# Transposing the packed queries of six batches with one crossbar transfer in place of twelve PE transposes

## The chip, the cores and the metric

One core of a Trainium2 chip. The metric is device time of one execution in microseconds (us), less is better; medians are over single executions, and each execution also reports the mean clock that was granted to TensorE (1.00 is full speed). "PE" is TensorE's matmul side, DVE VectorE, ACT ScalarE, POOL GpSimd, SP the engine whose queue issues the output writes and the crossbar transposes here. A "crossbar transfer" is here a DMA that transposes bf16 data on its way from SBUF to SBUF. A transfer has landed with the last of its sixteen semaphore updates in the trace (counted here as one for each DMA engine).

## The reference, cut to what matters

```python
# q, k, v: (8, 8, 576, 64); p: (8, 8, 32, 64)  (batch, heads, sequence, head size)
p_packed = sm_attn(p, k, v)            # 32 packed queries attend to 576 keys
out      = sm_attn(q, p_packed, p_packed)   # 576 queries attend to 32 packed rows
x = out.transpose(0, 2, 1, 3).reshape(4608, 512)
h = x @ w_in; g = h * np.cos(h); result = g @ w_out      # 512 -> 2048 -> 512
```

For the first product the kernel needs p transposed, head size on the partitions: this is the tile `P2`, for all eight batches. It is a small tensor (8 x 8 x 32 x 64).

## The kernel before

The kernel is a software pipeline over batches. Slot `s` does the feed-forward part of batch `s` (16 steps `fc` of `h_mm`), fills PE with output matmuls of batch `s-1` ("fillers"), and runs pieces of the attention of the next batches as hooks at given steps. All this is one stream of PE instructions.

```python
    def xbar(n, b):                                   # q or k of batch b, by the crossbar
        t = xT[n, b] = att_pool.tile([128, H * 3, TP], BF16, ..., bufs=2 if n == "k" else 1)
        nc.sync.dma_start_transpose(out=t, in_=bf[n, b].rearrange("p h x -> p (h x)"))

    def pack_p(b0, b1, flat=None):                    # p of batches b0..b1-1, by PE
        ng = 2 * (b1 - b0)
        if flat is None:
            flat = psa(BF16).rearrange("p a x -> p (a x)")
        for g in range(ng):
            nc.tensor.transpose(flat[:, g * 128:(g + 1) * 128],
                                p_bf[:, 2 * b0 + g].rearrange("p t d -> p (t d)"), ident)
        V.tensor_copy(out=P2[:, b0:b1].rearrange("p b h n -> p (b h n)"), in_=flat[:, 0:ng * 128])

    # a1_xbar(b): crossbar transfer of the softmax weights a1 of batch b -> a1T[b]
    # pp(b):      PE product of a1T[b] with v of batch b; ppw(b, n): its product with w_in
    # [cut]
    def next_loads():
        G.tensor_copy(out=gate, in_=xT["k", 3][0:1, 0, 0:1])     # POOL waits until kT of batch 3 is there
        for n, b in (("q", 3), ("k", 4), ("v", 3)):
            load(n, b)

    # [cut]
    load("q", 2)
    load("k", 3)
    dup_p(4, 2 * B, G)                                # POOL casts p to p_bf
    # [cut]
    slot(1, [(3, lambda: pw2(1, 2, (ACT, V))), (4, lambda: (xbar("q", 2), xbar("k", 3))), (5, tk("k", 2, 0)), (6, tk("k", 2, 1)),
             (7, tk("k", 2, 2)), (9, lambda: pack_p(2, 5)),
             (11, lambda: pack_p(5, B)), (12, next_loads)], 4, {3: 3})
    # [cut]  s1(2), pp(2), s2(2), s1(3), then:
    xbar("q", 3)
    a1_xbar(3)
    recips(3)
    xbar("k", 4)
    # [cut]
    slot(2, [(7, lambda: pp(3, engs=(ACT, ACT))), (11, lambda: pw2(3))], 5, {11: 3})

    for s in range(3, B):                             # [cut] the same chain, once per slot
        ...
        slot(s, [(5, lambda: pp(s + 1, engs=(ACT, ACT))), (10, lambda: pw2(s + 1))] if nxt else [], 5, {10: 3})
```

The softmax here doesn't subtract the row's maximum and nothing guards it: scores larger than these inputs give would overflow.

## Time and profile before

| | before |
|---|---|
| time, median of 6 runs | 248.92 us (248.79 to 249.83) |
| span of the profiled run, granted clock | 247.7 us, 1.00 |
| PE busy | 236.7 us, 96% of the span |
| chain of waits that ended last | 74% PE, 15% DMA (first weights) |

From the profile's page: the busy row of all engines, then two of the rows that cut the span into 40 slices (a digit is tenths of busy time; PEclk is the granted clock), then the chain of waits by engine.

```profile
PE 236.7 (96%) x2037; PEld 131.4 (53%) x2037; DVE 167.3 (68%) x253; ACT 166.8 (67%) x278; POOL 57.8 (23%) x70
...
PEclk9999999999999999999999999999999999999999
DMA  5999999999899989999998985999481113101133
...
PE 74%; DMA 15%; DVE 4%; ACT 2%; POOL 2%; issue 1%; DVEq 0%; POOLq 0%
```

PE is the bound. The DMA engines show work in flight nearly all the time up to 150 us, though they are hardly on the chain after 44 us. The two PE places that matter are in PE's timeline (columns: start in us, time in us, engine, line, operation, count; a bracket at the end of a line would be idle time ahead of it):

```profile
56.06 0.65 PE L256 MATMUL psA<-a2n,PPW 128*128 128x288 bf16 x4
56.55 0.50 PE L117 MATMUL psA<-ident,p_bf 128*128 128x128 bf16 x6
56.88 0.59 PE L309 MATMUL ot<-w_out_bf,gT 128*128 128x512 bf16 x2
57.53 0.65 PE L256 MATMUL psA<-a2n,PPW 128*128 128x288 bf16 x4
...
84.42 0.38 PE L309 MATMUL ot<-w_out_bf,gT 128*128 128x512 bf16 x1
84.63 0.65 PE L256 MATMUL psA<-a2n,PPW 128*128 128x288 bf16 x4
85.19 0.86 PE L183 MATMUL psA<-a1T,vp 96*128 96x64 bf16 x24
85.89 0.60 PE L309 MATMUL ot<-w_out_bf,gT 128*128 128x512 bf16 x2
```

The first four lines are step 9 of slot 1: with six transposes (L117) the step takes 57.53 - 56.06 = 1.47 us, where a plain step with two fillers takes 0.92. The last four are pp(3) (L183) in slot 2: no idle time ahead of it. Its first weight load, which overlaps the matmuls before it, starts at 85.00:

```profile
85.00 0.92 PEld L183 LDWEIGHTS <-vp 96*128 96x128 bf16 x24
```

The data for pp(3) comes down the SP queue; its timeline:

```profile
47.64 2.05 SPq L316 DMA_DIRECT2D out_dram<-osb  x4
56.42 3.92 SPq L93 DMA_TRANSPOSE qT<-qbf  x1
60.39 2.94 SPq L93 DMA_TRANSPOSE kT<-kbf  x1
63.43 8.02 SPq L316 DMA_DIRECT2D out_dram<-osb  x6
72.82 6.16 SPq L93 DMA_TRANSPOSE qT<-qbf  x1
79.08 3.56 SPq L156 DMA_TRANSPOSE a1T<-a  x1
82.72 3.10 SPq L93 DMA_TRANSPOSE kT<-kbf  x1
```

The queue sits idle from 49.69 to 56.42, until the load of q2 lands. And POOL's timeline, for the two events that frame this stretch: the cast of p, and the gate that holds back the next loads until kT of batch 3 has landed.

```profile
46.82 1.60 POOL L342 CAST p_bf<-p_raw 128x768 bf16<-128x768 f32 x2 [5.67 <-DMA p_raw<-in_p_dram]
...
65.36 0.18 POOL L443 COPY gate<-kT 1x1 bf16<-1x1 bf16 x1 [8.68 <-DMA kT<-kbf]
```

So there is a second chain beside PE: crossbar of k3 -> gate -> load of q3 -> crossbar of q3 (72.82) -> crossbar of a1 of batch 3 (79.08, its last semaphore update at 84.66) -> pp(3) on PE. It arrives only 0.3 us before PE wants it (84.66 against 85.00).

### The profile page before, as it was taken

The page shows a single profiled execution, that of the slowest core. Times are in us where ns is not written, and L with a number is a line of the kernel's source. Part 1 is how long each engine was busy: PE and PEld are TensorE (multiplying, and loading weights), DVE is VectorE, ACT ScalarE, POOL GpSimd, SP SyncE. Part 2 cuts the span into 40 slices and gives each one's busy share as a digit, 9 for nine tenths or more (in the row PEclk, how much of TensorE's full clock was granted, in tenths as well). Part 3 has the DMA queues.
Part 4 walks back from the last instruction along what each step waited for, and adds up shares of the span by engine and source line. Part 5 has one row for each costly group of instructions (what it writes and reads, how often), then busy time and mean ns, then how long its engine had stood idle before and what let it go on. Part 6 is the DMA issues. An engine that isn't in the chain of part 4 may idle for free.

```text
span 247.7 us, 5071 instructions
## 1 busy us (share of the span) xinstructions
PE 236.7 (96%) x2037; PEld 131.4 (53%) x2037; DVE 167.3 (68%) x253; ACT 166.8 (67%) x278; POOL 57.8 (23%) x70
## 2 busy tenths in 40 slices
PE   8888799999999999999999999999999999999993
PEld 3454374566554654565446554565456554665452
DVE  2449987789667977678767766678766684886110
ACT  2359789756656887888776777888777684873000
POOL 8252543240310455013404005030500000000000
PEclk9999999999999999999999999999999999999999
DMA  5999999999899989999998985999481113101133
GB/s 79 203 202 205 205 206 229 197 241 147 176 186 207 181 146 219 216 204 160 233 185 171 188 178 71 200 165 187 105 154 30 45 42 83 46 27 58 47 83 85
DMA packets 63175, 37.09 MB, mean 150 GB/s; under 512 B 35792, under 2 KB 58576, under 8 KB 63152
## 3 DMA queue, kind: packets, MB, share of 16 engines
q0 software_dynamic: 23152, 18.75, 49.8%
q1 hardware_dynamic: 39568, 17.83, 34.6%
q8 instruction: 16, 0.26, 0.4%
q10 hardware_dynamic: 432, 0.20, 0.4%
q14 instruction: 7, 0.06, 0.1%
HBM read 37.22 MB, written 9.44 MB: 188 GB/s over the span
## 4 chain that ended last, share of the span: by engine, by line
PE 74%; DMA 15%; DVE 4%; ACT 2%; POOL 2%; issue 1%; DVEq 0%; POOLq 0%
PE ot L309 44%; PE psA L256 20%; DMA w_out_bf<-in_moe_w_out_dram 9%; DMA w_in_bf<-in_moe_w_in_dram 7%; PE psA L207 3%; DVE gT L263 2%; PE psA L129 2%; PE psA L183 2%; PE ot L295 1%; ACT cosT L260 1%; PE psA L233 1%; DVE PPW L77 1%; ACT ppT L75 1%; DVE a2n L243 1%; POOL kbf L84 1%
## 5 line engine op out<-in xcount | busy, mean ns | idle before, releaser
L309 PE MATMUL ot<-w_out_bf,gT 128*128 128x512 bf16 x512 | 133.3, 379 | 0.1
L263 DVE TENSOR_TENSOR gT<-psA,cosT 128x576 bf16<-128x576 f32 x128 | 93.7, 756 | 26.6 <-ACT cosT L260 25.9
L260 ACT ACTIVATE cosT<-psA 128x576 bf16<-128x576 f32 x128 | 82.5, 652 | 27.7 <-PE psA L256 24.5
L256 PE MATMUL psA<-a2n,PPW 128*128 128x288 bf16 x512 | 83.9, 286 | 1.4 <-DVE PPW L77 0.4
L309 PEld LDWEIGHTS <-gT 128*128 128x128 bf16 x512 | 47.7, 98 | 43.3 <-issue 6.8
L256 PEld LDWEIGHTS <-PPW 128*128 128x128 bf16 x512 | 49.3, 98 | 34.7 <-issue 3.9
L77 DVE CAST PPW<-psA 128x1024 bf16<-128x1024 f32 (+1 forms) x23 | 26.9, 1176 | 11.6 <-PE psA L207 11.5
L267 POOL COPY joint<-gT 128x512 bf16<-128x512 bf16 x16 | 9.9, 616 | 85.5 <-DVE gT L263 85.5
L77 DVE COPY osb<-ot 128x512 f32<-128x512 f32 (+1 forms) x24 | 16.3, 679 | 17.5 <-PE ot L309 13.9
L77 POOL COPY vp<-vbf 96x3072 bf16<-96x3072 bf16 x7 | 19.3, 2751 | 5.1 <-DMA vbf<-in_v_dram 5.1
L75 ACT COPY osb<-ot 128x512 f32<-128x512 f32 (+1 forms) x13 | 7.3, 565 | 15.3 <-PE ot L309 10.6
L243 DVE SCALAR_TENSOR_TENSOR a2n<-a2u,r,lns 128x576 bf16<-128x576 bf16 x16 | 12.4, 813 | 7.3 <-ACT lns L241 7.3
L235 ACT ACTIVATE lns<-psA 128x576 f32<-128x576 f32 x16 | 10.1, 650 | 7.1 <-PE psA L233 6.5
L140 ACT ACTIVATE a<-psA 128x576 bf16<-128x576 f32 x16 | 10.3, 647 | 6.7 <-PE psA L129 6.7
L309 PE MATMUL ot<-w_out_bf,joint 128*128 128x512 bf16 x48 | 13.0, 379 | 0.0
L225 ACT ACTIVATE a2u<-psA,rs 128x576 bf16<-128x576 f32 x16 | 11.0, 737 | 1.4 <-PE psA L129 1.2
L75 ACT CAST ppT<-psA 64x128 bf16<-64x128 f32 x24 | 6.2, 260 | 6.5 <-DVE ppT L77 5.9
L207 PE MATMUL psA<-w_in_bf,ppT 64*32 64x512 bf16 x224 | 10.2, 381 | 0.0
L241 ACT ACTIVATE lns<-lns 128x576 f32<-128x576 f32 x16 | 10.0, 676 | 0.0
L347 PE MATMUL ot<-wz 128*128 128x512 bf16 x25 | 8.7, 486 | 1.2 <-DVE wz L358 1.2
L84 POOL DMA_DIRECT2D vbf<-in_v_dram x8 | 6.2, 777 | 6.8 <-DVE vp L77 4.8
L77 DVE COPY kT<-psA 128x768 bf16<-128x768 bf16 x8 | 4.2, 552 | 5.1 <-PE psA L104 5.0
(73 smaller groups left out, 150.4 us busy)
## 6 DMA issues: line engine op xcount, KB each, us to landing
kbf<-in_k_dram POOLq DMA_DIRECT2D x8, 576.0 KB, 12.7
vbf<-in_v_dram POOLq DMA_DIRECT2D x8, 576.0 KB, 7.8
qbf<-in_q_dram POOLq DMA_DIRECT2D x8, 576.0 KB, 10.0
out_dram<-osb SPq DMA_DIRECT2D x24, 192.0 KB, 2.5
out_dram<-osb SPq DMA_DIRECT2D x22, 128.0 KB, 2.4
w_in_bf<-in_moe_w_in_dram POOLq DMA_DIRECT2D x4, 512.0 KB, 17.5
w_out_bf<-in_moe_w_out_dram POOLq DMA_DIRECT2D x4, 512.0 KB, 21.2
out_dram<-osb SPq DMA_DIRECT2D x26, 64.0 KB, 2.1
```

The source lines that it names most:

```text
L75: ACT.copy(out=out, in_=in_)
L77: eng.tensor_copy(out=out, in_=in_)
L140: ACT.activation(out=a1[b % 2][:, y, :, 0:TP].rearrange("p (e m) x -> p e m x", e=2), in_=ps[y][:, :, 0:HS].rearrange("p e (m x) -> p e m ...
L207: nc.tensor.matmul(ps[y][32 * x:32 * x + 32, :], ppT[b % 2][r, 2 * x + y, :], w_in_bf[r, x, n * 512:(n + 1) * 512], start=True, stop=True)
L225: ACT.activation(out=a2u[b][:, y].rearrange("p (e x) -> p e x", e=2), in_=ps[y][:, :, 0:HS], func=AF.Exp, scale=rs1[b][:, y:y + 1])
L235: ACT.activation(out=lns[b][:, y].rearrange("p (e x) -> p e x", e=2), in_=ps[:, :, 0:HS], func=AF.Ln)
L241: ACT.activation(out=lns[b][:, y], in_=lns[b][:, y], func=AF.Exp, scale=-1.0)
L243: V.scalar_tensor_tensor(out=a2n[b][:, y], in0=a2u[b][:, y], scalar=r1[b][:, y:y + 1], in1=lns[b][:, y], op0=ALU.mult, op1=ALU.mult)
L256: nc.tensor.matmul(ps[:, e, 0:HS], PPW[b][:, y, fc * 128:(fc + 1) * 128], a2n[b][:, y, e * HS:(e + 1) * HS], start=(y == 0), stop=(y == 1))
L260: ACT.activation(out=csv, in_=ps[:, :, 0:HS], func=AF.Sin, bias=PI_HALF)
L263: V.tensor_tensor(out=gT[b][:, fc, :].rearrange("p (e x) -> p e x", e=2), in0=ps[:, :, 0:HS], in1=csv, op=ALU.mult)
L309: nc.tensor.matmul(pss[c], w, w_out_bf[:, fc, :], start=(fc == 0), stop=(fc == NFC - 1))
```

## The change

p is to be transposed by one crossbar transfer (128 x 1536 elements) in the idle stretch of the SP queue, so that PE is rid of twelve transposes and DVE of two copies from PSUM.

```diff
+    def xbars():
+        nc.sync.dma_start_transpose(
+            out=P2[:, 2:B].rearrange("p b (g h) n -> p (b g) (h n)", g=2),
+            in_=p_bf[:, 4:2 * B].rearrange("p g t d -> p (g t d)"))
+        xbar("q", 2)
+        xbar("k", 3)
+
@@
-    slot(1, [..., (4, lambda: (xbar("q", 2), xbar("k", 3))), (5, tk("k", 2, 0)), (6, tk("k", 2, 1)),
-             (7, tk("k", 2, 2)), (9, lambda: pack_p(2, 5)),
-             (11, lambda: pack_p(5, B)), (12, next_loads)], 4, {3: 3})
+    slot(1, [..., (4, xbars), (5, tk("k", 2, 0)), (6, tk("k", 2, 1)),
+             (7, tk("k", 2, 2)), (12, next_loads)], 4, {3: 3})
```

More of the change, by code (lines that the diff above doesn't have):

```diff
@@ L461 @@
     fill(14)
-    slot(1, [(3, lambda: pw2(1, 2, (ACT, V))), (4, lambda: (xbar("q", 2), xbar("k", 3))), (5, tk("k", 2, 0)), (6, tk("k", 2, 1)),
-             (7, tk("k", 2, 2)), (9, lambda: pack_p(2, 5)),
-             (11, lambda: pack_p(5, B)), (12, next_loads)], 4, {3: 3})
+    slot(1, [(3, lambda: pw2(1, 2, (ACT, V))), (4, xbars), (5, tk("k", 2, 0)), (6, tk("k", 2, 1)),
+             (7, tk("k", 2, 2)), (12, next_loads)], 4, {3: 3})
     ACT.preload_act_table_set(EXP_SET)
```

## The prediction

> **What bounds the kernel now.** The page's busy table has PE at 236.7 us of 247.7 (96%), clock 1.00; the chain of waits is 74% PE, 15% DMA (weight loads before 44 us), 4% DVE. After 44 us PE work counts one to one, unless PE then meets a wait. The DMA row reads 9 in nearly every slice up to 150 us. Beside PE runs a DMA chain with little slack: k's crossbar, the next three loads (gated by kT), q's crossbar, a1's crossbar, pp.
>
> **What goes.** Twelve PE transposes in two hooks of slot 1 (fc 9 and 11). The timeline shows 0.50 us for six of them, and two 0.55 us evictions of P on DVE. Steps with such a hook take 1.47 and 1.52 us, the same without 0.92 us. So PE saves about 1.1 us near 58 to 60 us, on the chain.
>
> **What comes.** One crossbar transfer, 128 x 1536 bf16, an a1 crossbar's size, which the SP timeline shows 1.43 us issuing when quiet, 3.56 us under load; 4.0 us to land. Its source is ready: POOL's cast of p ends at 48.4. The SP queue is idle from 49.7 to 56.42, where q2's crossbar waits for q2's load (waits of the SP queue). So no issue is delayed. s1(2) needs P2 at 64.4; it should land by 60.
>
> The cost is bandwidth. From 44 to 57 us the loads run at a steady 265 packets of 768 B per us: saturated. The new transfer is 1536 packets of 256 B; the trace's crossbars move 800 to 1130 such packets per us alone: I estimate 1.4 to 1.9 us more of all 16 engines ahead of q2's and k3's crossbars. [...] at 77 to 78.5 us, beside crossbar packets, loads fall from 133 to about 90 per half microsecond. Some hides in gaps near 58.5 and 61 us. I take kT3 to land 0.7 to 2 us late (now 65.1), centre 1.3.
>
> **On the critical path.** kT3 itself has 7 us of slack before s1(3) at 72.0. But the next loads are gated by it (POOL waits until 65.36); q3's crossbar issues when q3 lands (72.8), a1's follows at 79.08 and lands near 84.7; pp(3) starts at 85.0. Slack: 0.3 us. With PE 1.1 us earlier and a1T 1.3 us later, PE should stall there about 2 us. Net: -1.1 + (1.1 + 1.3 - 0.3) = +1.0 us. At pp(4) slack exceeds 1 us: nothing more is lost.
>
> **Predicted time: 249.8 us, 248.0 to 251.3** (8 in 10). Faster by over 2%: 0.01; within 2%: 0.96; slower by over 2%: 0.03.
>
> **What would show each step.** Transposes of p on PE down from 16 to 4, steps fc 9 and 11 at 0.92 us; s1(2) near 63.3 instead of 64.39. The new transpose issued near 49.7, issuing for 2 to 4 us; q2's crossbar about 1 us after 56.42. POOL's gate 0.7 to 2 us after 65.36. An idle gap on PE of 1 to 3 us before pp(3), released by the a1T DMA; pp(3) near 86. From there both traces run parallel.
>
> **What would make it wrong.** If the new transfer fits into DMA gaps, the delay is near zero and the kernel gains up to 1 us (248). If it stalls q2's crossbar longer, the loss is 2 to 3 us.

One clause of the recorded text is cut (marked), as no trace of this case shows it. What the trace of the kernel before has: "saturated" is a DMA share of 1.27 (packet times, as a share of 16 engines' time) at 213 GB/s from 44 to 57 us; 768 B packets started at 244 to 270 per us from 45 to 51 us and from 54 to 56, but at 104 to 174 per us between, beside output writes, so they were not steady throughout. "Quiet" is a share of 0.59 during the issue of 1.43 us (at 155.84), "under load" 1.30 during that of 3.56 us (at 79.08). The slack at pp(4) is 1.5 us (a1T of batch 4 lands at 107.46, pp(4) starts at 108.98).

## The result, and the profile after

| | before | after |
|---|---|---|
| time, median of 6 runs | 248.92 us | 252.45 us |
| range | 248.79 to 249.83 | 250.65 to 254.83 |
| single runs after, with granted clock | | 250.65 (1.000); 252.18, 252.35, 252.56, 252.82 (0.993); 254.83 (0.987, slow) |
| ratio | | 1.012, 95% interval 1.0085 to 1.0156 |

A ratio is the mean time of one kernel's runs over the mean of the other's in the same rounds, so it is not quite the ratio of the medians. Executions over 1.5% slower than the fastest of the same kernel are left out of the means. The change made the kernel 1.2% slower, and outside the predicted range. Already the list of runs is telling: the times stand in steps, and each step goes with a clock. The page of the profiled run after (250.4 us, clock 0.993), the same rows as above:

```profile
PE 237.4 (95%) x2025; PEld 131.4 (52%) x2025; DVE 166.2 (66%) x251; ACT 166.7 (67%) x278; POOL 57.7 (23%) x70
...
PEclk9999999999999979999999999999999999999999
DMA  6999999999999989999999992999381112202133
...
PE 79%; DMA 12%; DVE 3%; ACT 2%; issue 1%; POOL 1%; DVEq 0%; POOLq 0%
```

PE has twelve instructions fewer and yet is busy 0.7 us longer; PEclk has a 7 in its fifteenth slice. PE's timeline, the same two places:

```profile
56.46 0.65 PE L256 MATMUL psA<-a2n,PPW 128*128 128x288 bf16 x4
56.95 0.59 PE L309 MATMUL ot<-w_out_bf,gT 128*128 128x512 bf16 x2
57.38 0.65 PE L256 MATMUL psA<-a2n,PPW 128*128 128x288 bf16 x4
...
82.97 0.65 PE L256 MATMUL psA<-a2n,PPW 128*128 128x288 bf16 x4
86.33 0.86 PE L183 MATMUL psA<-a1T,vp 96*128 96x64 bf16 x24 [2.70 <-DMA a1T<-a]
87.02 0.67 PE L309 MATMUL ot<-w_out_bf,gT 128*128 128x512 bf16 x2
87.48 1.17 PE L256 MATMUL psA<-a2n,PPW 128*128 128x288 bf16 x4
```

The steps of slot 1 are down to 0.92 us. But ahead of pp(3) PE now stands idle for 2.70 us, released by the a1T transfer; and the next group of four matmuls (L256) takes 1.17 us where it took 0.65. The view by windows shows why (columns: window and its length; busy us and count of PE, PE weight loads, DVE, ACT, POOL; granted clock; DMA share; GB/s):

```profile
84.00:87.42 3.42, 1.09 (x26) 0.93 (x27) 1.10 (x2) 0.51 (x2) 0.45 (x1) 1.00 1.09 226
87.42:90.84 3.42, 3.42 (x13) 1.82 (x12) 0.85 (x2) 2.14 (x6) 1.05 (x3) 0.50 0.78 178
```

For the 3.41 us from 87.42 on, the clock was 0.50, so PE got 1.7 us less done. The SP queue and POOL after:

```profile
47.12 2.05 SPq L316 DMA_DIRECT2D out_dram<-osb  x4
49.22 4.20 SPq L443 DMA_TRANSPOSE P<-p_bf  x1
57.52 4.19 SPq L93 DMA_TRANSPOSE qT<-qbf  x1
61.81 3.08 SPq L93 DMA_TRANSPOSE kT<-kbf  x1
64.99 5.04 SPq L316 DMA_DIRECT2D out_dram<-osb  x6
74.43 6.93 SPq L93 DMA_TRANSPOSE qT<-qbf  x1
81.46 1.46 SPq L156 DMA_TRANSPOSE a1T<-a  x1
83.01 4.30 SPq L93 DMA_TRANSPOSE kT<-kbf  x1
```

```profile
46.17 1.60 POOL L342 CAST p_bf<-p_raw 128x768 bf16<-128x768 f32 x2 [5.40 <-DMA p_raw<-in_p_dram]
...
66.89 0.18 POOL L450 COPY gate<-kT 1x1 bf16<-1x1 bf16 x1 [10.73 <-DMA kT<-kbf]
```

The new transfer (49.22) went out in the idle stretch and was issued by 53.42; q2's crossbar still waited until 57.52, and not for the queue but for the load of q2. The start of a run jitters by some tenths (here 0.65 us earlier), so I measure from the cast of p to the gate: 65.36 - 46.82 = 18.54 us before, 66.89 - 46.17 = 20.72 us after. The chain is 2.2 us late. The packets of this trace, counted by their start in half microseconds (768 B packets are loads, 256 B crossbar, 2048 B output writes), show the stretch ahead of q2's crossbar:

```
start   768 B   256 B  2048 B
50.0     130       0       0      loads alone
52.0      61       0      48      the four output writes share
54.0      93      97       0      the new transfer shares
55.5      18      25       0      near-standstill
56.0      18      16       0      near-standstill
57.0      95      93       0
```

So far this shows where the time went: +1.7 us in the half clock, and +2.7 us in the gap, against 1.1 us saved. The new transfer itself landed at 61.76, 12.5 us after its issue, and 1.0 us before s1(2) reads it (62.73), so nothing waited for P2. All this doesn't show that the gap caused the half clock, nor which part of the new transfer is to blame.

### The profile page after: what moved, and what is told of

It is laid out like the page before. It is cut to its first block, busy times and chain, and to the rows that moved or that the text cites. A ratio compares the mean times of both kernels' runs of the same rounds, so it can differ in the third digit from the quotient of the medians.

```text
span 250.4 us, 5047 instructions
## 1 busy us (share of the span) xinstructions
PE 237.4 (95%) x2025; PEld 131.4 (52%) x2025; DVE 166.2 (66%) x251; ACT 166.7 (67%) x278; POOL 57.7 (23%) x70
## 4 chain that ended last, share of the span: by engine, by line
PE 79%; DMA 12%; DVE 3%; ACT 2%; issue 1%; POOL 1%; DVEq 0%; POOLq 0%
PE ot L309 47%; PE psA L256 22%; DMA w_in_bf<-in_moe_w_in_dram 7%; DMA vbf<-in_v_dram 3%; PE psA L207 3%; PE psA L129 2%; DMA a1T<-a 2%; PE psA L183 2%; PE psA L233 1%; PE ot L295 1%; DVE gT L263 1%; ACT cosT L260 1%; DVE PPW L77 1%; ACT ppT L75 1%; DVE a2n L243 1%
## 5 line engine op out<-in xcount | busy, mean ns | idle before, releaser
L256 PE MATMUL psA<-a2n,PPW 128*128 128x288 bf16 x512 | 85.0, 288 | 1.2 <-DVE PPW L77 0.4
L256 PEld LDWEIGHTS <-PPW 128*128 128x128 bf16 x512 | 49.8, 99 | 35.0 <-issue 3.7
L235 ACT ACTIVATE lns<-psA 128x576 f32<-128x576 f32 x16 | 10.1, 649 | 7.1 <-PE psA L233 6.5
L183 PEld LDWEIGHTS <-vp 96*128 96x128 bf16 x192 | 6.5, 98 | 4.5 <-issue 3.5
L183 PE MATMUL psA<-a1T,vp 96*128 96x64 bf16 x168 | 6.0, 193 | 2.9 <-DMA a1T<-a 2.7
```

What stands on the lines that cost most here:

```text
L183: nc.tensor.matmul(ps[:, hp * 64:(hp + 1) * 64], vp[b][:, c, hp * 128:(hp + 1) * 128], a1T[b][0:TP, :, j, 32 * hp:32 * hp + 32], start=(j ...
L235: ACT.activation(out=lns[b][:, y].rearrange("p (e x) -> p e x", e=2), in_=ps[:, :, 0:HS], func=AF.Ln)
L256: nc.tensor.matmul(ps[:, e, 0:HS], PPW[b][:, y, fc * 128:(fc + 1) * 128], a2n[b][:, y, e * HS:(e + 1) * HS], start=(y == 0), stop=(y == 1))
```

## The experiments

Twelve kernels ran, in three groups of four, each group on one chip with its own runs of the kernel before (249.16, 248.86 and 248.88 us median, 11 runs each). All were recorded as correct, `no_xbar` too, whose P2 is a constant for six of the eight batches. With these inputs the check can't see a wrong P2: the reference, computed again with p at 0.01 in those batches, changes by 0.2% of its norm. So nothing shows that the new transfer puts its data in the right places; the times don't depend on that. "Theory A" is that the gap halves the clock.

### fill12 and fill6: cover the gap

```diff
-    def pp(b, own=False, engs=(V, ACT)):
-        ps = bank() if own else psa()[:, 0, :]
+    def pp(b, own=False, engs=(V, ACT), dummies=0):
+        two = None if own else psa()
+        ps = bank() if own else two[:, 0, :]
+        for _ in range(dummies):
+            nc.tensor.matmul(two[:, 1, :], wz[:, 0:128], wz, start=True, stop=True)
@@ slot 2 of the changed kernel
+    pp(3, engs=(ACT, ACT), dummies=12)      # fill6: 6
```

> The changed kernel with 12 dummy matmuls (zeros, 128x512) ahead of pp(3), into the unused half of pp's own PSUM tile: the wait for a1T stays, PE is busy through it. Theory A (the 2.7 us of idle PE before pp(3) make the clock fall to half in the next window): the clock stays 1.00 in all runs, time about 250.7 us, 1.7 us less than the changed kernel's usual 252.4. Rival B (the clock falls because of the denser load of PE or DMA, not because of the gap): clock still 0.993, 252.4 us or more.

> The same with 6 dummies, so about 1.3 us of the 2.7 us gap is covered and 1.4 us stays idle. Theory A: a gap this short is harmless (the kernel before had gaps of up to 1.1 us at clock 1.00), so clock 1.00 and 250.7 us. If even this gap halves the clock: 252.4 us.

Measured: fill12 250.78 us (clock 0.997 to 1.000 in all six runs; ratio to the kernel before 1.0071), fill6 250.60 us (five runs, ratio 1.0058; in the profiled one the clock was 0.990, from a half-clock window at 32 us, in the start-up, not here). PE's timeline of fill12, then of fill6:

```profile
83.52 2.75 PE L182 MATMUL psA<-wz 128*128 128x512 bf16 x12
86.44 0.86 PE L186 MATMUL psA<-a1T,vp 96*128 96x64 bf16 x24 [0.17 <-DMA a1T<-a]
...
85.08 1.46 PE L182 MATMUL psA<-wz 128*128 128x512 bf16 x6
86.37 0.86 PE L186 MATMUL psA<-a1T,vp 96*128 96x64 bf16 x24
```

In fill12 pp(3) starts as late as without the dummies (86.44 against 86.33), so the wait is all there; only the idleness is gone, and with it the half clock and 1.7 us. Theory A holds, and rival B (denser work) falls: fill12 is the denser kernel. The trace of fill6 doesn't show what a gap of 1.4 us does. PE had lost time to the start-up window and came to pp(3) 1.4 us later than in fill12, counted from the cast of p, so that the six dummies left no idle time at all. Its time of 250.54 us is no longer than those of the four runs at full clock (250.23 to 251.14): what PE had lost was hidden in the wait for a1T. That these four, which have no trace, had the 1.4 us gap is likely and not shown. fill12 also shows the loss without the clock: 250.8 - 249.2 = 1.6 us, which is the gap of 2.7 less the 1.1 saved.

### early_before: the gap without the change

```diff
@@ kernel before
-    slot(2, [(7, lambda: pp(3, engs=(ACT, ACT))), (11, lambda: pw2(3))], 5, {11: 3})
+    slot(2, [(3, lambda: pp(3, engs=(ACT, ACT))), (11, lambda: pw2(3))], 5, {11: 3})
```

> The kernel before, with no transfer of p at all, but pp(3) moved from step 7 to step 3 of slot 2, so that PE comes to it about 3 us before a1T lands: the same gap, made without the change. Theory A (an idle PE halves the clock in the next window): gap of 2 to 3 us before pp(3), clock 0.993 in most runs, about 249.0 + 2.5 + 1.7 = 253.2 us. Rival B (the transfer or the denser PE work makes the clock fall): clock 1.00 and 251.5 us.

Measured: 253.41 us (four runs: three at clock 0.993, 253.40 to 253.98; one at 1.000, 251.97).

```profile
84.79 0.86 PE L183 MATMUL psA<-a1T,vp 96*128 96x64 bf16 x24 [2.89 <-DMA a1T<-a]
...
82.12:85.53 3.41, 0.74 (x24) 0.77 (x26) 1.33 (x2) 0.47 (x1) 0.90 (x1) 1.00 1.20 250
85.53:88.94 3.41, 3.19 (x16) 1.73 (x14) 0.76 (x1) 1.74 (x6) 0.42 (x2) 0.50 0.92 193
```

(The first line is from the timeline, the other two from the view by windows.) The same gap, made in the old kernel by nothing but an earlier step for pp(3), gives the same half clock. The transfer is not needed for it.

### extra_xbar: the cost alone

```diff
@@ kernel before: PE transposes kept
+    P_scr = const.tile([128, B - 2, H, NP], BF16, name="P_scr")     # nobody reads it
+    # ahead of xbar("q", 2):
+        nc.sync.dma_start_transpose(
+            out=P_scr.rearrange("p b (g h) n -> p (b g) (h n)", g=2),
+            in_=p_bf[:, 4:2 * B].rearrange("p g t d -> p (g t d)"))
```

> The kernel before with its twelve PE transposes kept, and the same crossbar transfer ahead of q2's, into a scratch tile that nobody reads. The cost alone. Theory: q2, kT3 and a1T3 land 1.5 to 2 us later than before; PE saved nothing, so the gap at pp(3) is 1.2 to 1.7 us and the time 250.5 us with the clock at 1.00, up to 252.3 in runs where it falls. Rival (the loss comes from P2 arriving late at s1(2), or from the new order on PE): 249.0 us, since neither is in this kernel.

Measured: 250.55 us, median of four scattered runs (249.22 and 250.11 at clock 1.000, 250.99 and 252.77 at 0.993; ratio 1.0078, interval 1.0039 to 1.0118). Gate minus cast is 20.74 us, the 2.2 us delay in full. The loss comes with the transfer alone. In the profiled run the gap at pp(3) was only 0.61 us, less than expected: PE had itself lost time to a half-clock window at 31.7 us. Whether the scatter of the other runs comes from such start-up windows is open, as only one run of each kernel has a trace.

### no_xbar: the saving alone (wrong result)

```diff
@@ changed kernel
-        nc.sync.dma_start_transpose(out=P2[:, 2:B]..., in_=p_bf[:, 4:2 * B]...)
+    G.memset(P2[:, 2:B], 0.01)              # once, at the start
```

> The changed kernel without the crossbar transfer (batches 2 to 7 of P2 hold a constant: the result is wrong on purpose). The saving alone. If PE's 1.1 us came through whole: 247.9 us. My theory: the DMA chain is as in the kernel before, a1T3 lands at the same time, so PE meets it with a gap of about 0.8 us at pp(3) and only 0.3 us of the saving is left: 248.7 us, clock 1.00.

Measured: 248.43 us (five runs, 248.16 to 248.66; ratio 0.9983, interval 0.9971 to 0.9995), gap at pp(3) 0.74 us. Had the transfer been free, the change would have gained 0.4 us, not 1.1: the remainder of the saving ends in the wait for a1T, which nobody has made earlier.

### behind_k3: the same transfer at another place

```diff
@@ changed kernel, xbars()
-        nc.sync.dma_start_transpose(out=P2[:, 2:B]..., in_=p_bf[:, 4:2 * B]...)
         xbar("q", 2)
         xbar("k", 3)
+        nc.sync.dma_start_transpose(out=P2[:, 3:B]..., in_=p_bf[:, 6:2 * B]...)
@@ slot 1
+             (9, lambda: pack_p(2, 3)),
```

> The changed kernel with the transfer moved from ahead of q2's crossbar to behind k3's, for batches 3 to 7 only; batch 2 is packed by two PE transposes at step 9, as s1(2) needs it at once. Theory: q2 and k3 are not delayed, the gate for the next loads opens as in the kernel before, the transfer runs in the DMA lull before those loads; PE keeps about 0.6 us of saving, of which 0.3 us gets past pp(3): 248.7 us, clock 1.00. Rival (the bytes themselves cost, wherever they go): 250 us or more.

Measured: 252.20 us (ratio 1.0125, interval 1.01 to 1.015), clock 0.993 in four of six runs. My expectation fell, and the time is the rival's. The gate did open as before (18.48 us after the cast), yet q3's crossbar then issued 10.1 us after the gate, against 7.5 us before. The trace shows the load of q3 landing on 13 of the 16 DMA engines between 71.4 and 72.8 us and on the last three at 73.8, 74.5 and 74.8; q3's crossbar issued at 74.87, once the last had landed. The fourth output write of this stretch, which had landed by 67.6 us in the kernel before, straggles likewise: its pieces landed between 69.3 and 74.7 (the last three at 73.2, 73.6, 74.7), in the midst of the loads. The gap at pp(3) was 2.50 us. That this collision is the cause was read from one trace, not tested.

### half and plain_copy: bytes, or the crossbar

```diff
@@ half: changed kernel, six PE transposes kept
-            out=P2[:, 2:B]..., in_=p_bf[:, 4:2 * B]...
+            out=P2[:, 5:B]..., in_=p_bf[:, 10:2 * B]...
+             (9, lambda: pack_p(2, 5)),
@@ plain_copy: extra_xbar with an ordinary copy of the same 393 KB
-        nc.sync.dma_start_transpose(out=P_scr..., in_=p_bf[:, 4:2 * B]...)
+        nc.sync.dma_start(out=P_scr.rearrange("p b h n -> p (b h n)"), in_=p_bf[:, 4:2 * B]...)
```

> The changed kernel with only batches 5 to 7 in the crossbar transfer (768 packets in place of 1536) and batches 2 to 4 packed by six PE transposes at step 9. The gate for the next loads opened 18.2 to 18.6 us after the cast of p began in five traces without the transfer and 20.4 to 20.7 us in five with it: 2.2 us. If the delay is bytes alone: 1.1 us, so 19.5. If about 1 us of it is a fixed cost of one more crossbar starting under loads (near-standstill of all packets for 1 us at 55.5 in the changed kernel's trace): 1.6 us, so 20.0. PE saves about 0.55 us; gap at pp(3) 1.3 to 1.9 us, time 249.7 to 250.3 us at clock 1.00, up to 252 in runs where the clock falls.

> The run 'extra_xbar' with a plain copy of the same 393 KB in place of the crossbar transfer, same queue, same place, same scratch tile. If any 393 KB cost the same, gate minus cast is 20.6 us and the time is about 250.5 us. If it is the crossbar's small packets and its standstill, then a plain copy delays the gate by 1 us or less: 19.0 to 19.4 us, gap at pp(3) under 1 us, time 249.3 us.

Measured: half 249.67 us (ratio 1.0022, interval 1.0007 to 1.0036), clock 0.998 or more in all four runs, gap 1.33 us. plain_copy 248.93 us, ratio 1.000, no gap.

```profile
46.35 1.60 POOL L342 CAST p_bf<-p_raw 128x768 bf16<-128x768 f32 x2 [5.53 <-DMA p_raw<-in_p_dram]
66.42 0.18 POOL L450 COPY gate<-kT 1x1 bf16<-1x1 bf16 x1 [10.10 <-DMA kT<-kbf]
```

```profile
46.00 1.60 POOL L342 CAST p_bf<-p_raw 128x768 bf16<-128x768 f32 x2 [5.22 <-DMA p_raw<-in_p_dram]
65.41 0.18 POOL L452 COPY gate<-kT 1x1 bf16<-1x1 bf16 x1 [9.35 <-DMA kT<-kbf]
```

(First half, then plain_copy.) Gate minus cast is 20.07 us for half and 19.41 for plain_copy, against 18.24 to 18.55 in five traces that have nothing ahead of q2's crossbar (before, late_before, early_before, no_xbar, behind_k3), and 20.43 to 20.74 in five with the whole transfer there (after, fill12, fill6, late, extra_xbar). So half the crossbar transfer costs 1.6 to 1.7 us, three quarters of the whole one's 2.2: bytes alone would be 1.1. And a plain copy of all the bytes costs 1.0 at the gate, of which 0.2 is left when a1T lands (38.03 us after the cast, 37.85 in the kernel before). The packet counts point to the fixed part: about 2 us after its first packets, in half, in fill12, in late and in extra_xbar just as in the changed kernel, everything on the DMA engines nearly stops for 0.7 to 1 us (after, from 55.5 to 56.5: 38 GB/s, against 193 in the 2 us ahead of it). Each is one trace per kernel; the spread within the two groups of five is 0.3 us.

### late and late2: let PE come later instead

```diff
@@ changed kernel (late_before: the kernel before)
-    slot(2, [(7, lambda: pp(3, engs=(ACT, ACT))), (11, lambda: pw2(3))], 5, {11: 3})
+    slot(2, [(10, lambda: pp(3, engs=(ACT, ACT))), (13, lambda: pw2(3))], 5, {13: 3})
@@ late2, in addition
+        f1, f2 = (8, 12) if s == 3 else (5, 10)
+        slot(s, [(f1, lambda: pp(s + 1, engs=(ACT, ACT))), (f2, lambda: pw2(s + 1))] if nxt else [], 5, {f2: 3})
```

> The changed kernel with pp(3) moved from step 7 to step 10 of slot 2, and the ppw pair behind it from 11 to 13, about 2.8 us later on PE. Theory A: a1T has landed (86.2 us in the profile), no gap, clock 1.00; what is left is the 1.1 us saved on PE: 247.8 us, a little faster than before. If the loss sits elsewhere (bandwidth taken from other transfers, other waits): 249 us or more.

> Control: the kernel before with the same move of pp(3) and ppw. It had no wait at pp(3), so 248.9 us. If the move alone is worth something, it shows here, and the gain of the run 'late' has to be counted against it.

> The run 'late' with pp(4) moved too, from step 5 to step 8 of slot 3, and its ppw pair from 10 to 12. Theory: the 2.2 us by which the transfer delays the DMA chain stay in that chain, so that in 'late' they came out again at pp(4) (gap 1.7 us at 109 us, clock halved at 112 us in 3 of 6 runs). With both later than a1T: no gap over 0.9 us, clock 1.00 in nearly all runs, about 248.2 us. Rival (the debt only moves on to pp(5) or shows elsewhere): 250 us again, with a gap later in the trace.

Measured: late_before 249.38 us (ratio 1.001, interval 0.9993 to 1.0028: the move itself is worth nothing). late 251.88 us: three runs at 250.2 to 250.8 with clock 1.000 and three at 253.0 to 253.6 with 0.993. My expectation fell. In the profiled run, one of the slower three, pp(3) still waited 0.87 us, and the main wait had moved on, to pp(4) of slot 3.

```profile
111.18 0.86 PE L183 MATMUL psA<-a1T,vp 96*128 96x64 bf16 x24 [1.74 <-DMA a1T<-a]
...
108.94:112.35 3.41, 1.67 (x33) 1.20 (x31) 1.81 (x3) 1.18 (x4) 0.00 (x0) 1.00 1.12 202
112.35:115.76 3.41, 3.41 (x14) 1.74 (x12) 1.41 (x2) 2.08 (x5) 0.00 (x0) 0.50 0.60 136
```

The wait that PE was partly spared at pp(3) came one batch later, as the chain was still late: a1T of batch 4 landed 64.2 us after the cast of p, against 60.5 in late_before. late2 ran from 247.85 to 253.07 us (median 249.82), with clock 0.998 or more in every run, two of them called slow for their time alone; the fast four have ratio 1.0009 (interval 0.9982 to 1.0036), so they win back the loss and no more. One run got the whole saving, as expected; the others didn't. The only trace of late2 is of a slow run, and speaks for that run alone. It has gaps of 2.30 us at pp(3) and 1.61 us ahead of pp(5) (the view names DVE there; a1T landed at the same 138.21 us): q3's crossbar issued 10.1 us after the gate again, for a load of q3 that was on 15 engines by 74.1 us and on the last at 76.9. So in that run the delay wandered on, as the rival said, and a load was much later than the transfer makes it. Why one engine lags in some runs stays open.

### stage3: a version for both

```diff
@@ kernel before
-             (11, lambda: pack_p(5, B)), (12, next_loads)], 4, {3: 3})
+             (12, next_loads)], 4, {3: 3})
@@ slot 2: pp(3) at step 8 in place of 7; in the loop over s, behind xbar("k", s + 2):
+                if s == 3:
+                    nc.sync.dma_start_transpose(
+                        out=P2[:, 5:B].rearrange("p b (g h) n -> p (b g) (h n)", g=2),
+                        in_=p_bf[:, 10:2 * B].rearrange("p g t d -> p (g t d)"))
```

> A version meant to beat both: batches 2 to 4 packed by PE at step 9 as before, batches 5 to 7 by a crossbar transfer in stage 3, behind k5's crossbar (near 108 us), where a1T lands some 5 us ahead of pp(5); pp(3) one step later. P2[5] is first needed at 121 us. Saves one hook of slot 1, about 0.55 us, with the DMA chain of slots 1 and 2 untouched: 248.3 us, clock 1.00. If the transfer costs there what it cost in slot 1, it eats slack and no time. Rival (a crossbar transfer costs PE time wherever it goes): 249 us or more.

Measured: 248.37 us (five runs, 248.26 to 248.53, clock 0.997 or more; ratio 0.9977, interval 0.9965 to 0.9989).

```profile
108.02 1.29 SPq L526 DMA_TRANSPOSE P<-p_bf  x1
```

Half of the transposes taken off PE, their transfer put where pp has slack (in the kernel before, a1T of batch 5 lands at 130.11 and pp(5) starts at 135.07): 0.5 us faster than before, about what six transposes cost PE. It is the better version of the idea, worth 0.2%.

## Why the prediction was wrong

- Right: PE's saving. The steps with transposes went from 1.47 and 1.52 us to 0.92; s1(2) came 1.0 us earlier relative to the cast of p (64.39 - 46.82 = 17.57 us before, 62.73 - 46.17 = 16.56 us after).
- Right: the place and the mechanism. The chain kT -> gate -> q3 -> a1T -> pp(3) was delayed, had next to no slack, and PE stalled at pp(3), released by the a1T DMA. extra_xbar, no_xbar and the profile after agree.
- Wrong, but without effect: the new transfer was to take 4.0 us to land and be there by 60. It took 12.5 us and landed at 61.76, still ahead of s1(2).
- Off in size: the term "kT3 to land 0.7 to 2 us late, centre 1.3". It was 2.2 us between the means of five traces with the transfer (20.62) and five without (18.40). The delay reached the end of the chain: a1T of batch 3 landed 39.7 to 40.6 us after the cast in the five with the transfer, and 37.7 to 38.2 in the five without, behind_k3 with its late q3 load (40.2) apart. I had costed packets at the crossbar's rate; half and plain_copy point to a part of it that doesn't shrink with the bytes; the near-standstill would fit it. That made the gap 2.7 us in place of 2 and the loss 1.6 to 1.7 us in place of 1.0: the one run at full clock, 250.65 us, lies inside my range.
- The step that failed: "Net: -1.1 + (1.1 + 1.3 - 0.3) = +1.0 us", which counts an idle gap of PE at its own length. The runs showed a second term, 1.7 us: the clock at half for one window of 3.41 us after the gap. Its place is seen in the one run with a trace; four more runs have the same or a lower mean clock (0.993, 0.987) and are 1.7 us or more above the one at full clock. fill12 (gap covered, wait kept: 250.8 us, clock 0.997 or more in all six runs) and early_before (gap made without the change: half clock again) show that the gap is the cause; fill6 (250.6 us) agrees, as far as its trace goes. It carried the median out of the range.

I had predicted a gap of 1 to 3 us and didn't ask what it does to the clock.

The traces of all fourteen kernels show more closely which gaps were followed by a half clock. Every trace ends in a half-clock stretch (before: PE's last matmul ends at 243.65, the half clock starts at 248.28; after: 246.45 and 251.26). In each of the six traces with another one inside the kernel, the two starts lie a whole number of windows apart, a window being the 3.413 us that the half clock inside the changed kernel lasted (after: 251.26 - 87.42 = 163.84 = 48 windows). So I laid a grid of such windows through every trace. For each window after the first 5 us, the share in which no matmul ran (their ends are modelled), from the worst down:

| window, from us | PE idle in it | next window at half clock? |
|---|---|---|
| early_before, 82.12 | 78% | yes |
| behind_k3, 83.79 | 73% | yes |
| after, 84.01 | 68% | yes |
| late, 108.94 | 51% | yes |
| fill6, 28.64 (start-up) | 49% | yes |
| late2, 134.95 | 49% | no |
| extra_xbar, 28.29 (start-up) | 44% | yes |
| late2, 87.16 | 42% | no |
| half, 84.17 | 41% | no |
| late_before, 27.20 (start-up) | 39% | no |

No other window was more than 38% idle, and none of those was followed by a half clock. The table leaves out the end of each trace, where PE runs out of work. There, as far as the traces go on, every window at full clock that was idle for 60% or more was followed by a half clock, also where PE still worked in the rest of it (late_before, from 242.24: 60%), and the others, up to 47% (late, from 245.47), were not. So in these traces every window idle for 51% or more led to a half clock and none up to 43% did; in between it went both ways (44% and one of 49% did, 47% and the other 49% didn't). About half a window of idleness was enough here, not a whole one. The gap of 2.3 us in late2 (86.25 to 88.55; a run called slow for its time, at full clock) fits: a boundary at 87.16 cut it in two. That the grid falls differently in each run would also explain why the same kernel pays in some runs and not in others; that is argued, as one run of each kernel has a trace.

## What to carry to other kernels

Cost an idle gap of PE at its length plus a possible 1.7 us of half clock when it can fill about half of a 3.4 us window (here, every window idle for 51% or more was followed by one); twelve dummy matmuls in front of the wait bought that back here (252.45 to 250.78 us). Before moving work from the bound engine to DMA, find the DMA chain that feeds the bound engine and measure its slack: an idle issue queue is not idle bandwidth (here, SP's idle stretch from 49.69 to 56.42 us had a DMA share of 1.25 and 235 GB/s), and work taken off PE gains nothing that the next wait for DMA takes back (no_xbar: 0.4 us came through of 1.1). Move such work to a stage with slack in that chain, as stage3 did, and don't expect to win by only consuming later: in late the delay stayed in the chain and came out at the next batch, and late2 was no faster than the kernel before.

## What else the traces showed, and what stays open

- A gap of 1.74 us (late, 51% of its window) was followed by a half clock, and 2.30 us split over two windows (late2) was not: in these traces it is the idle share of one window, with the limit between 43% and 51%, that decided. Each half-clock stretch inside the kernels lasted one window, 3.413 us, after which PE, busy again, had its full clock.
- Next to running loads the same 393 KB delayed the next gate by 1.0 us as a plain copy and by 2.2 us through the crossbar.
- All DMA packets came near a standstill for 0.7 to 1 us about 2 us after the new crossbar transfer began under loads, in five traces (after: 18 + 25 packets per half microsecond, against 86 + 88 just before). The mechanism is open.
- The sixteen engines of one load finished far apart in behind_k3: three of them were done with q3 up to 2 us after the other thirteen. Why is open too.
